# Which engine makes the first softmax-sum addition: a routed attention and mixture-of-experts kernel with one addition per group on GpSimd, an earlier transpose and one more drain

## The chip, the cores and the metric

One NeuronCore of a Trainium2 chip runs the whole kernel as one program. The metric is the device time of one execution in microseconds (us), taken as the median of several executions. The engines are TensorE (PE, with its weight loads as PEld), VectorE (DVE), ScalarE (ACT), GpSimd (POOL) and SyncE (SP, which here only issues DMAs). Each engine works through its own queue in order and waits on semaphores for the others.

## The reference

```python
# attention: 4 batches, 8 heads, 768 positions, head width 64, 16 clusters
q_assign = np.argmax(np.einsum('bhsd,hcd->bhsc', q_n, c_n), axis=-1)
k_assign = np.argmax(np.einsum('bhsd,hcd->bhsc', k_n, c_n), axis=-1)
mask = q_assign[:, :, :, None] == k_assign[:, :, None, :]
scores = np.where(mask, scale * np.matmul(q, k.transpose(0, 1, 3, 2)), -1e9)
attn = np.exp(scores - np.max(scores, axis=-1, keepdims=True))
attn = attn / (np.sum(attn, axis=-1, keepdims=True) + 1e-09)
x = heads_side_by_side(np.matmul(attn, v))                  # 3072 x 512

# router and experts: 8 experts, 512 -> 1024 -> 512
logits = xn @ en.T / tau
expert_idx = np.argmax(logits, axis=1)
gate_w = softmax(logits)[np.arange(N), expert_idx]
for e in range(E):
    mask = expert_idx == e
    h = np.maximum(x[mask] @ w1[e], 0.0)
    out[mask] = gate_w[mask, None] * (h @ w2[e])
```

A position attends only to the keys of its own cluster, and each of the 3072 rows goes through one expert.

## The kernel before

The order of instructions on all five engines is written out by hand: the program's order is the order of each queue.

**Attention** is done for 16 pairs of heads (4 batches, 4 pairs each, `n` from 0 to 15). A pair has two groups (the halves `hq` of its 768 queries) and a group has six units (`j`, 128 keys each). A unit's scores are computed by `scores` into a PSUM tile of two, `expo` exponentiates them on ACT into one of five `prob` buffers (128 x 768 values), and `attend` multiplies them with `v` into `o_ps`. The main loop takes two units at a time, so a pair has six iterations `it` (0 to 2 for the first group, 3 to 5 for the second). In each iteration the scores and exponentials of the next two units come before the attention products of the current two. An exponential therefore needs the buffer of the unit five places earlier, which both `attend`'s matmuls and its addition must have read.

The denominators are collected beside this. `attend` adds the `prob` tiles of a group up into `acc`: for `j == 1` one DVE instruction (L515) adds the first two and a small constant, and for each later unit another DVE instruction (L525) adds one more. When a group ends, ACT copies `o_ps` into `o_sb` (L530, one buffer), and `unite` adds its two halves into `o_sum` (L539) on POOL, in the last pair on DVE. This is done in iteration 2 for a pair's first group and in iteration 5 for its second. In iteration 0 of the next pair `total` (L553) sums `acc` over partitions on PE for both groups, and DVE and POOL turn and copy the reciprocals (L570, L571, L574). In iteration 2 `divide` transposes them (L585) and scales `o_sum` into `xT` (L589). `rows` (L606, L613) turns `xT` and writes it to memory in iteration 3.

Other work stands between these: the next pair's transposes of q and k (L386), its cluster choice (L405, L414 to L417, with ACT's L419 and L422), a batch's router products, logits and choice (L632, L644, `choose` from L680 on, with six small additions on POOL for running counts, L686), and, from batch 2 on, the placement of the rows of the first four expert blocks (`early`, for instance L864, L747, L931 and L934, and three gathers issued by POOL in iteration 3 of pair 14).

**Behind attention** the last batch's router runs between the first expert blocks. `products(0)` (L632, for the first half of the batch) is issued at the end of the loop, `products(1)` after the last group has been divided. Their results lie in PSUM tiles that `misc()` hands out in turn from two, and `logits` (L644) transposes each into `lt` on DVE. `total` of the last group takes the other tile between them. Then the experts follow: four early blocks, and 16 more items, `sized` ones (32-row pieces, gathered and scattered by POOL's indirect DMAs, L1041 and L1052) and blocks of 128 rows in turn. The last item is a block. Ahead of it `send` scatters the pieces of the sized item before it, and its own result is scattered last (L1288 on ACT, then L1052). At the end of the program every engine drains and meets the others.

Of the kernel before, what the change touches and what calls it, by code (L numbers as in the profile page):

```python
# [12 lines left out]
ALU = mybir.AluOpType  # L13
# [21 lines left out]
def bc(ap, shape, axis):  # L35
    return ap.unsqueeze(axis).to_broadcast(shape)
# [3 lines left out]
def kernel(  # L40
# [12 lines left out]
    nc = tc.nc  # L53
# [8 lines left out]
    HS = S // 2  # L62
# [118 lines left out]
    NP = len(pairs)  # L181
# [277 lines left out]
    un = [dict() for _ in units]  # L459
# [32 lines left out]
    def expo(i):  # L492
        d = un[i]
        d["prob"] = probs[i % len(probs)]
        nc.scalar.activation(d["prob"][:, :, 0:HS], d["s_ps"][:, :, 0:HS], ACTF.Exp, scale=scale)  # L495

    def attend(i):

        n, hq, j = units[i]
        d, g = un[i], gr[i // GU]  # L500
        if j == 0:
            g["o_ps"] = psO.tile([P, 2, 512], F32, tag="o_ps", name="o_ps")
        for h in range(2):
            for half in range(2):
                keys = slice(D * half, D * half + D)
                nc.tensor.matmul(  # L506
                    g["o_ps"][D * h : D * h + D, half, 0:HE],
                    lhsT=ld[n]["v"][keys, j, h],
                    rhs=d["prob"][keys, h, 0:HE],
                    start=(j == 0),  # L510
                    stop=(j == NJ - 1),
                )
        if j == 1:
            g["acc"] = xp.tile([P, 2, HS], F32, tag="acc", name="acc", bufs=3)
            nc.vector.scalar_tensor_tensor(  # L515
                out=g["acc"],
                in0=un[i - 1]["prob"][:, :, 0:HS],
                scalar=NJ * EPS,
                in1=d["prob"][:, :, 0:HS],
                op0=ALU.add,  # L520
                op1=ALU.add,
            )
            un[i - 1].clear()
        elif j > 1:
            nc.vector.tensor_tensor(g["acc"], g["acc"], d["prob"][:, :, 0:HS], ALU.add)  # L525
            d.clear()
        if j == NJ - 1:
            t = ld[n]
            t["o_sb"] = xp.tile([P, 2, HE], F32, tag="o_sb", name="o_sb", bufs=1)
            nc.scalar.copy(t["o_sb"], g["o_ps"][:, :, 0:HE])  # L530

    def unite(g):

        n, hq, _ = units[GU * g]
        t = ld[n]
        if hq == 0:
            t["o_sum"] = xp.tile([P, 2, HE], F32, tag="o_sum", name="o_sum", bufs=2)
        add = (nc.gpsimd if n + 1 < NP else nc.vector).tensor_tensor
        add(t["o_sum"][:, hq], t["o_sb"][:, 0], t["o_sb"][:, 1], ALU.add)  # L539
# [38 lines left out]
    def divide(*gs):  # L578
        n, hq, _ = units[GU * gs[0]]
        d = gr[gs[0]]  # L580
        G = len(gs)
        if hq == 0:
            xT[pairs[n]] = xp.tile([P, 2, HS], F32, tag="xT", name="xT", bufs=4)
        if G == 2:
            nc.vector.transpose(  # L585
                d["den"].rearrange("p k (u t) -> p (k u) t", t=SQ),
                bc(d["inv2"].rearrange("p k h u -> p (k h u)"), [P, G * HS // SQ, SQ], 2),
            )
        nc.vector.scalar_tensor_tensor(  # L589
            out=xT[pairs[n]][:, hq : hq + G],  # L590
            in0=ld[n]["o_sum"][:, hq : hq + G, 0:HS],
            scalar=ld[n]["o_sum"][:, hq, HS:HE],
            in1=d["den"],
            op0=ALU.add,
            op1=ALU.mult,
        )
        for g in gs:
            gr[g].clear()
# [486 lines left out]
    def weights2(it, parts=1):  # L1085
        for i in range(parts):
            load_part(w2s[it.slot], moe_w2, it.e, KF, i, parts)
# [152 lines left out]
    def send(it):  # L1240

        u0 = FIRST[it.j]
        for u in range(WIDE[it.j]):
            at = flat(spidx)[:, u0 + u : u0 + u + 1]
            scatter(out_pieces, at, mo[it]["ys"][:, u], NQ * N)
        del mo[it]

    def flat(t):
        return t.rearrange("p k w -> p (k w)")

    def hidden(it, halves=(0, 1)):

        d = mo[it]
        for half in halves:
            if half == 0:
                d["hT"] = mop.tile([P, F], F32, tag="hT", name="hT")
            f0 = 512 * half
            bk = psH.tile([P, 512], F32, tag="h_ps", name="h_ps")
            for m in range(0, 512, P):
                for c in range(KD):  # L1260
                    nc.tensor.matmul(  # L1261
                        bk[:, m : m + P],
                        lhsT=w1s[it.slot][:, c, f0 + m : f0 + m + P],
                        rhs=d["xT"][:, P * c : P * c + P],
                        start=(c == 0),
                        stop=(c == KD - 1),
                    )
            nc.scalar.activation(d["hT"][:, f0 : f0 + 512], bk, ACTF.Relu)  # L1268
# [133 lines left out]
    with tc.manual_schedule(engines=by_hand):  # L1402
        begin()
        for i in range(0, len(units), 2):
            n, it = divmod(i // 2, NJ)

            if n == it == 0:
                load(2, "qk")
            if it == 2 and n + 1 < NP:
                load(n + 1, "v")  # L1410
            if it >= 4 and n + 3 < NP:
                load(n + 3, "qk"[it - 4])
            for m in range(i + 2, min(i + 4, len(units))):
                scores(m)
                expo(m)
            between(n, it)
            if it == 4 and n == NP - 1:
                divide(2 * n)
            b, nb = divmod(n, NHP)
            if (b, nb, it) in early:  # L1420
                early[b, nb, it]()
            if i + 2 == len(units):
                ats.close()
                tile_waits = {"side": "right", "reuse_waits": "tile"}
                psX = ctx.enter_context(tc.tile_pool(name="psX", bufs=1, space=PSUM, **tile_waits))
                turn_x(E0[0], nc.scalar.copy, xp.tile([P, DM], F32, tag="acc", name="xTm", bufs=3))
            for m in range(i, i + 2):
                attend(m)
            if it == 2:
                if n > 0:  # L1430
                    divide(2 * n - 2, 2 * n - 1)
                unite(2 * n)
            elif it == 5:
                unite(2 * n + 1)
            if i + 2 == len(units):
                rows(ngroups - 2)
                route[b][0](0)
            if it == 0 and n > 0:
                total(2 * n - 2, 2 * n - 1)
            elif it == 3 and n == NP - 1:  # L1440
                total(2 * n)
# [10 lines left out]
        products, logits, read, norms, choose = route[B - 1]  # L1452
        pb = Places(1, rtb)
        gates = gate_pieces(0, B - 1)
        gates[0]()
        hidden(E0[0], (0,))
        order_x(E0[3])
        total(ngroups - 1)
# [7 lines left out]
        hidden(E0[0], (1,))  # L1466
        gates[3]()
        weights1(E0[2])
        logits(0)
        read(0, NJ, P - SQ, P)  # L1470
        products(1)
        hidden(E0[1], (0,))
# [82 lines left out]
        LAST = len(later) - 1  # L1555
        for i, it in enumerate(later):
            if i == LAST - 1:
                overflow()
                weights1(later[LAST])
                weights2(later[LAST])  # L1560
            if it.kind == "sized":
                order_w2(it)
            if i + 1 < len(later):
                turn_x(later[i + 1])
            if i > 0 and i + 2 < len(later) and later[i + 2].kind == "sized":
                fetch(later[i + 2])
            if i > 0 and later[i - 1].kind == "sized":
                send(later[i - 1])
            if it.kind == "sized":
                sized_hidden(it)  # L1570
            else:
                hidden(it)
            if i == 0:
                pb.gates(slot_gates)
            for j in range(i + 2, min(i + 4, len(later))):
                if later[j].kind == "block" and later[j] not in mo:
                    if it.kind == "sized":
                        nc.gpsimd.tensor_copy(pace, mo[it]["hT"][0:1, KF - 1, 0:1])
                        fetch(later[j])
            if i + 2 < LAST:  # L1580
                weights1(later[i + 2])
                if it.kind == "sized":
                    weights2(later[i + 2])
            if it.kind == "sized":
                sized_result(it)
            else:
                result(it)
            if i == 0:
                fetch(later[2])
                spread_gates()  # L1590
            if i + 2 < LAST and it.kind != "sized":
                weights2(later[i + 2])
# [45 lines left out]
```

## Time and profile before

| | us |
|---|---|
| median of 8 runs | 709.48 (709.26 to 710.89) |
| the profiled execution | 709.55 |
| its span, first to last instruction | 707.8 |
| PE busy in the span | 690.8 (98%) |
| DVE busy | 382.4 (54%) |
| ACT busy | 265.1 (37%) |
| POOL busy | 267.8 (38%) |
| granted TensorE clock, mean | 0.995 |

A row of a group names line, engine, operation, out<-in, partitions x elements and count, then busy time, mean ns of one, and the idle time of the engine before it with what ended it. A row of the timeline begins with the start and the duration in us; the brackets hold the idle time before it and its releaser. A table by stage gives, for each stretch, its length, the busy time of PE, PEld, DVE, ACT and POOL, the granted clock (1.00 is full), the share of the DMA engines and GB/s. An engine's name with a q is its sequencer, which waits, drains or issues. The mean shares hide the stages: attention runs to about 335 us, with DVE busy for 17 to 19 of every 20 us, and the experts from there to the end, with DVE mostly idle.

### The profile page before, as it was taken

To read this page: it belongs to the slowest core of one execution; us is meant where nothing else is said; L and a number is where in the kernel's file an instruction comes from. 1 tells how busy PE (TensorE), PEld (TensorE's weight loads), DVE (VectorE), ACT (ScalarE), POOL (GpSimd) and SP (SyncE) were. 2 spreads that over 40 slices of the span, in tenths; PEclk is the share of its full clock that TensorE was granted. 3 is DMA by queue.
4 is the path that set the end of the run, shared out by engine and by line. 5 is a ranking of instruction groups with operands and counts; after the bars stand their busy time and mean duration, and the time that the engine had idled before them with its cause. 6 is when DMAs were issued, how large, how long until landed. Compare 5 with 4: busy or idle time off the path is not lost.

```text
span 707.8 us, 16122 instructions
## 1 busy us (share of the span) xinstructions
PE 690.8 (98%) x6518; PEld 456.3 (64%) x6518; DVE 382.4 (54%) x665; ACT 265.1 (37%) x446; POOL 267.8 (38%) x402
## 2 busy tenths in 40 slices
PE   6999999999999999999899999999999999999995
PEld 3444444444444444455876668897979797979793
DVE  4788888989889999989484121340220303031210
ACT  4566655677566755576215110101011111111110
POOL 2122222322234222453213546736264554544412
PEclk9999999999999999999999999999999999999999
DMA  9536565786657688769788987268768686969450
GB/s 146 92 62 107 105 104 89 142 165 112 99 107 139 128 144 156 186 173 321 200 283 300 353 307 270 73 239 286 259 223 298 209 302 226 319 244 328 144 193 28
DMA packets 244124, 135.55 MB, mean 192 GB/s; under 512 B 207808, under 2 KB 207810, under 8 KB 244044
## 3 DMA queue, kind: packets, MB, share of 16 engines
q1 hardware_dynamic: 237852, 121.28, 64.0%
q0 software_dynamic: 6016, 13.12, 5.3%
q8 instruction: 54, 0.88, 0.6%
q14 instruction: 26, 0.21, 0.1%
q10 hardware_dynamic: 176, 0.05, 0.0%
HBM read 115.92 MB, written 13.12 MB: 182 GB/s over the span
## 4 chain that ended last, share of the span: by engine, by line
PE 80%; DVE 7%; DMA 5%; issue 4%; POOL 1%; SPq 1%; ACT 0%; POOLq 0%; DVEq 0%; ACTq 0%
PE s_ps L484 18%; PE o_ps L506 15%; PE h_ps L1261 10%; PE y_ps L1277 10%; PE h_ps L1176 9%; PE y_ps L1213 5%; PE misc L1213 5%; DMA out_dram<-ys,spidx 3%; PE x_ps L1176 3%; DVE acc L525 3%; PE misc L553 2%; PE misc L396 2%; DMA x_rows<-xb 1%; PE misc L632 1%; DMA k<-in_k_dram 1%
## 5 line engine op out<-in xcount | busy, mean ns | idle before, releaser
L495 ACT ACTIVATE prob<-s_ps 128x768 f32<-128x768 f32 x192 | 153.7, 812 | 95.0 <-PE s_ps L484 82.1
L484 PE MATMUL s_ps<-qT,kT 64*64 64x384 f32 x1536 | 156.0, 482 | 0.0
L506 PE MATMUL o_ps<-prob,v 64*64 64x385 f32 x1536 | 142.0, 486 | 0.0
L525 DVE TENSOR_TENSOR acc<-acc,prob 128x768 f32<-128x768 f32 x128 | 125.5, 981 | 8.8 <-ACT cd L422 0.5
L506 PEld LDWEIGHTS o_ps<-prob,v 64*64 64x64 f32 x1536 | 54.6, 133 | 70.3 <-issue 58.5
L1261 PE MATMUL h_ps<-xTm,w1s 128*128 128x128 f32 x768 | 90.0, 278 | 0.0
L1261 PEld LDWEIGHTS h_ps<-xTm,w1s 128*128 128x128 f32 x768 | 89.0, 195 | 1.4 <-issue 1.0
L1222 DVE STREAM_TRANSPOSE ys<-y_ps 128x256 f32<-128x256 f32 (+4 forms) x16 | 6.7, 417 | 153.4 <-PE y_ps L1213 153.4
L539 POOL TENSOR_TENSOR o_sum<-o_sb 128x385 f32<-128x385 f32 x30 | 32.0, 1068 | 144.1 <-ACT o_sb L530 144.1
L1052 POOL DMA_INDIRECT out_dram<-ys,spidx x56 | 56.9, 1017 | 74.7 <-DVE ys L1236 59.8
L1277 PE MATMUL y_ps<-w2s,hT 128*128 128x512 f32 x192 | 84.5, 593 | 0.0
L484 PEld LDWEIGHTS s_ps<-qT,kT 64*64 64x64 f32 x1536 | 56.0, 133 | 38.1 <-issue 34.9
L1176 PE MATMUL h_ps<-xTs,w1s 128*128 128x272 f32 (+7 forms) x384 | 72.9, 346 | 1.1 <-ACTq L1537 1.1
L1176 PEld LDWEIGHTS h_ps<-xTs,w1s 128*128 128x128 f32 x384 | 66.6, 190 | 8.0 <-issue 2.4
L1268 ACT ACTIVATE hT<-h_ps 128x512 f32<-128x512 f32 x24 | 14.3, 596 | 148.0 <-PE h_ps L1261 148.0
L484 PE MATMUL s_ps<-hot 64*64 64x384 bf16 x768 | 64.7, 325 | 2.2 <-ACT prob L495 1.1
L574 POOL COPY inv<-inv 32x12 f32<-32x12 f32 x120 | 45.5, 379 | 54.6 <-DVE inv L571 50.2
L1041 POOL DMA_INDIRECT xs<-x_rows,gpidx x56 | 57.4, 1026 | 17.1 <-issue 16.8
L1277 PEld LDWEIGHTS y_ps<-w2s,hT 128*128 128x128 f32 x192 | 35.6, 190 | 40.2 <-issue 40.2
L484 PEld LDWEIGHTS <-hot 64*64 64x64 bf16 x768 | 23.6, 106 | 39.4 <-issue 38.3
L1213 PE MATMUL y_ps<-hTs,w2o 128*128 128x272 f32 (+7 forms) x256 | 48.0, 346 | 0.0
L1213 PE MATMUL misc<-hTs,w2o 128*128 128x272 f32 (+7 forms) x256 | 48.0, 346 | 0.0
(264 smaller groups left out, 680.1 us busy)
## 6 DMA issues: line engine op xcount, KB each, us to landing
w1s<-in_moe_w_dram SPq DMA_DIRECT2D x18, 2048.0 KB, 11.1
w2s<-in_moe_w_dram SPq DMA_DIRECT2D x18, 2048.0 KB, 13.5
v<-in_v_dram SPq DMA_DIRECT2D x128, 48.0 KB, 2.3
q<-in_q_dram SPq DMA_DIRECT2D x60, 96.0 KB, 3.8
k<-in_k_dram SPq DMA_DIRECT2D x60, 96.0 KB, 3.7
x_rows<-xb SPq DMA_DIRECT2D x60, 96.0 KB, 2.7
xr<-x_rows SPq DMA_DIRECT2D x9, 512.0 KB, 3.9
w1s<-in_moe_w_dram SPq DMA_DIRECT2D x4, 1024.0 KB, 9.9
```

Source lines behind the costliest of these rows:

```text
L484: nc.tensor.matmul(s_ps[D * half : D * half + D, h, 0:HS], lhsT=l[rows, half], rhs=r[rows], start=part == (1 if len(parts) < 2 else 0), st ...
L495: nc.scalar.activation(d["prob"][:, :, 0:HS], d["s_ps"][:, :, 0:HS], ACTF.Exp, scale=scale)
L506: nc.tensor.matmul(g["o_ps"][D * h : D * h + D, half, 0:HE], lhsT=ld[n]["v"][keys, j, h], rhs=d["prob"][keys, h, 0:HE], start=(j == 0), st ...
L525: nc.vector.tensor_tensor(g["acc"], g["acc"], d["prob"][:, :, 0:HS], ALU.add)
L539: add(t["o_sum"][:, hq], t["o_sb"][:, 0], t["o_sb"][:, 1], ALU.add)
L574: nc.gpsimd.tensor_copy(inv2[M * to : M * to + M, :, i % 2], inv[M * i : M * i + M])
L1041: nc.gpsimd.indirect_dma_start(out=to, out_offset=None, in_=of, in_offset=bass.IndirectOffsetOnAxis(ap=at, axis=0), bounds_check=n - 1, oo ...
L1052: inst = nc.gpsimd.indirect_dma_start(out=to, out_offset=bass.IndirectOffsetOnAxis(ap=at, axis=0), in_=of, in_offset=None, bounds_check=n - 1,
L1176: nc.tensor.matmul(bk, lhsT=w1s[it.slot][:, c, P * f : P * f + P], rhs=d["xT"][:, c, 0:C], start=(c == 0), stop=(c == KD - 1),)
L1213: nc.tensor.matmul(bks[g][:, 0:C], lhsT=d["w2"][:, f, P * g : P * g + P], rhs=d["hT"][:, f, 0:C], start=(f == 0), stop=(f == KF - 1),)
L1261: nc.tensor.matmul(bk[:, m : m + P], lhsT=w1s[it.slot][:, c, f0 + m : f0 + m + P], rhs=d["xT"][:, P * c : P * c + P], start=(c == 0), stop ...
L1277: nc.tensor.matmul(bk, lhsT=d["hT"][:, P * c : P * c + P], rhs=w2s[it.slot][:, c], start=(c == 0), stop=(c == KF - 1),)
```

## The change

There are three independent parts.

1. The first addition of each group is done by POOL and without the constant; the second addition, on DVE, takes the constant over. `unite` of a group is issued later: for the first group of a pair in iteration 3 instead of 2, for the second in iteration 0 of the next pair instead of iteration 5, each time behind POOL's first addition of the following group. The last pair keeps its old places.
2. `logits(0)` of the last batch is issued right after the first gate piece behind the loop, before `total` and `divide` of the last group, where it used to stand behind them and the other gate pieces.
3. One drain of POOL is issued ahead of the last item, behind the scatters of the sized item before it.

```diff
         if j == 1:
             g["acc"] = xp.tile([P, 2, HS], F32, tag="acc", name="acc", bufs=3)
+            nc.gpsimd.tensor_tensor(
+                g["acc"], un[i - 1]["prob"][:, :, 0:HS], d["prob"][:, :, 0:HS], ALU.add
+            )
+            un[i - 1].clear()
+        elif j == 2:
             nc.vector.scalar_tensor_tensor(
                 out=g["acc"],
-                in0=un[i - 1]["prob"][:, :, 0:HS],
+                in0=g["acc"],
                 scalar=NJ * EPS,
                 in1=d["prob"][:, :, 0:HS],
                 op0=ALU.add,
                 op1=ALU.add,
             )
-            un[i - 1].clear()
+            d.clear()
         elif j > 1:
             nc.vector.tensor_tensor(g["acc"], g["acc"], d["prob"][:, :, 0:HS], ALU.add)
             d.clear()
...
-            if it == 2:
-                if n > 0:
-                    divide(2 * n - 2, 2 * n - 1)
+            if it == 0 and n > 0:
+                unite(2 * n - 1)
+            if it == 2 and n > 0:
+                divide(2 * n - 2, 2 * n - 1)
+            if it == (3 if n + 1 < NP else 2):
                 unite(2 * n)
-            elif it == 5:
+            elif it == 5 and n + 1 == NP:
                 unite(2 * n + 1)
...
         gates[0]()
+        logits(0)
         hidden(E0[0], (0,))
         order_x(E0[3])
         total(ngroups - 1)
...
         weights1(E0[2])
-        logits(0)
         read(0, NJ, P - SQ, P)
         products(1)
...
             if i > 0 and later[i - 1].kind == "sized":
                 send(later[i - 1])
+                if i == LAST:
+                    nc.gpsimd.drain()
```

## The prediction

> **What bounds the kernel now.** I read the page's chain of waits first. It runs through TensorE for 80% of the span, so what counts is where PE waits, not how busy an engine is.
>
> ```profile
> PE 80%; DVE 7%; DMA 5%; issue 4%; POOL 1%; SPq 1%; ACT 0%; POOLq 0%; DVEq 0%; ACTq 0%
> ...
> L525 DVE TENSOR_TENSOR acc<-acc,prob 128x768 f32<-128x768 f32 x128 | 125.5, 981 | 8.8 <-ACT cd L422 0.5
> ...
> L539 POOL TENSOR_TENSOR o_sum<-o_sb 128x385 f32<-128x385 f32 x30 | 32.0, 1068 | 144.1 <-ACT o_sb L530 144.1
> ```
>
> Next, the timeline of a typical pair of heads in attention. `total` (L553) starts at 79.07 and again at 98.40 us, so a pair takes 19.33 us, and PE runs without a gap in it; DVE is busy for 17 of 20 us there but late for nobody on PE.
>
> ```profile
> 82.80 4.17 DVE L525 TENSOR_TENSOR acc<-acc,prob 128x768 f32<-128x768 f32 x4
> 83.93 1.56 ACT L495 ACTIVATE prob<-s_ps 128x768 f32<-128x768 f32 x2 [0.17 <-PE s_ps L484]
> ...
> 92.65 1.56 ACT L495 ACTIVATE prob<-s_ps 128x768 f32<-128x768 f32 x2 [0.98 <-PE s_ps L484]
> 94.37 1.98 DVE L525 TENSOR_TENSOR acc<-acc,prob 128x768 f32<-128x768 f32 x2
> ...
> 98.40 0.88 PE L553 MATMUL misc<-acc,ones 128*32 128x192 f32 x16
> ```
>
> Only two pairs are stretched: the L553 starts at 237.14, 257.89 and 279.39 are 20.75 and 21.50 us apart. Less 19.33, and less the batch's router products in the second (some 1.6), 1.4 and 0.6 us remain. There PE waits for `acc` or for `prob` that DVE holds. So 2.0 us is all that a faster DVE can win.
>
> Third, behind attention, the only place where PE stands still for long:
>
> ```profile
> 339.03 3.74 PE L1261 MATMUL h_ps<-xTm,w1s 128*128 128x128 f32 x32
> 344.55 0.24 DVE L644 STREAM_TRANSPOSE lt<-misc 128x96 f32<-128x96 f32 x1
> 344.85 0.87 PE L632 MATMUL misc<-xT,embT 128*32 128x96 f32 x32 [2.08 <-DVE lt L644]
> 345.64 5.47 PE L1261 MATMUL h_ps<-xTm,w1s 128*128 128x128 f32 x32
> ...
> 346.00:348.00 2.00, 2.00 (x12) 2.00 (x11) 1.19 (x7) 0.00 (x0) 0.52 (x3) 0.50 0.02 2
> ```
>
> The last row is from the table by stage; its third number from the end is the granted clock, 0.50. The same 32 matmuls take 3.74 us before the gap of 2.08 and 5.47 behind it: the gap costs a second time.
>
> Last, the end of the program:
>
> ```profile
> L1633 POOLq DRAIN  x3: 40/113/6020, 700.9 to 707.5; - x3
> L1633 SPq DRAIN  x3: 7/7/13, 704.5 to 707.2; - x3
> 701.14 0.97 POOL L1052 DMA_INDIRECT out_dram<-y,sidx  x1 [7.40 <-ACT y L1288]
> ```
>
> GpSimd's closing drain takes 6.02 us, 700.9 to 706.9. SP, which waits for all DMAs, is through at 704.5. So the drain alone sets the last 2.4 us.
>
> **Logits turned sooner.** `products(1)` (L632) takes the PSUM bank that `logits(0)` (L644) reads, and L644 stands last of DVE's queue there. In the instruction listing of the changed kernel it stands before the reciprocal L562. Its input is ready at 334.05; DVE finishes `xb` at 336.66 and is idle until 338.65, so the 0.24 us costs nothing (without that idle time, 0.24). It issues no DMA and is moved past no other queue. PE then waits for `xT` alone, written at 341.87, before its matmuls end at 342.77: -2.08 us. The half clock goes with the gap: 5.47 - 3.74 = -1.73. The weights PE comes to sooner leave slack: issued at 347.12, moved by 355 (the GB/s by stage), needed at 362.2. Sum -3.8, certain to some 0.3 if the clock stays up.
> [...] This trace shows 0.50 behind a gap of 2.08, and the trace decides.
>
> **First addition on GpSimd.** 32 DVE instructions (L515, 0.94 us each in 30.1 us) go; the next addition takes over the constant; 32 additions of 128x768 come onto POOL. Their price is not in the trace. From L539 (0.86 us alone for 385 columns): in proportion 1.72, with the 0.19 of the smallest copies as a fixed part 1.53; L934's 528 bf16 columns in 1.59 give 2.3 in proportion. I take 1.65, nearest to L539; ends 1.5 and 2.3.
> [...]
>
> Dearer than its duration is whom it stops:
>
> ```profile
> 76.06 0.96 DVE L525 TENSOR_TENSOR acc<-acc,prob 128x768 f32<-128x768 f32 x1
> 76.30 1.44 POOL L539 TENSOR_TENSOR o_sum<-o_sb 128x385 f32<-128x385 f32 x1 [7.79 <-ACT o_sb L530]
> ...
> 86.97 0.86 POOL L539 TENSOR_TENSOR o_sum<-o_sb 128x385 f32<-128x385 f32 x1 [2.94 <-ACT o_sb L530]
> ...
> 135.79 2.62 DVE L525 TENSOR_TENSOR acc<-acc,prob 128x768 f32<-128x768 f32 x2
> 136.72 0.86 POOL L539 TENSOR_TENSOR o_sum<-o_sb 128x385 f32<-128x385 f32 x1
> ```
>
> Beside a DVE addition POOL ends 0.72 after DVE (77.74 against 77.02); where POOL was first, DVE's addition ends 0.83 after POOL (138.41 against 137.58). At 86.97 DVE ran a transpose and POOL was undisturbed. So additions of the two engines take turns, and each collision costs DVE POOL's whole time.
>
> Second group of a pair (iteration 3): its first two `prob` are there at 85.49, amid DVE's four additions, so DVE loses 1.65 - 0.13 = 1.5 and gains 0.94. First group: ready at 94.21, just before DVE's last two. In the worst order the chain is 1.65 (POOL) + 0.83 + 0.72 (`unite`, now behind it) + 0.83 = 4.03, so `acc` is done at 98.24; PE asks for it at 98.40. It fits by 0.16: ordinary pairs cost nothing, and if that cover goes, each tenth costs 15 pairs x 0.1 = 1.5 us. What `unite` feeds (L589 at 87.9) is behind the transpose L585 and not late. The gathers of pair 14, which stood behind `unite`, come ahead of both on POOL: 3 x 1.3 us from `gidx` at 305.65, done by 309.6, with the addition done at 311.2, as late as L515 is now (311.4).
>
> Where POOL or DVE is fuller it does not fit. Pairs 5, 9 and 13 put six `cumx` additions (3.76 us from 211.87) ahead of it on POOL: it starts at 215.63, DVE's last addition is held to 217.2 and ends at 218.0 where PE asks at 217.81: 0.2 x 3 = 0.6. At the end of pair 10 DVE comes 0.5 late (1.5 - 0.94), the addition starts at 234.0 and holds back L864, L747 and both last additions: 235.65 + 0.14 + 0.72 + 0.8 + 1.9 = 239.2 against 237.59 now, 1.6. Pair 11 has the same again with L934 ahead on POOL, but PE is then late as well, so its own stall of 1.4 is what DVE's lateness first fills: I take 1.4 for both. Sum +2.0. Ends: -2.0 (the stalls go, nothing collides on the path) and +9 (POOL at 2.3: 0.48 x 15 + 2.0).
>
> **One more drain.** It stands behind the five scatters of the last sized block, issued by 693.74; POOL idles to 701.14. At 6.02 or less it hides there, and holds up only the last scatter, which waits for ACT until 700.9. Rows: 0.04 to 0.19 us for the drains with no DMA before them, 6.02 for the one behind all. If the closing drain must clear what all earlier scatters left, it shrinks and SP's end at 704.5 sets the finish: -2.4. If the 4.8 us behind the last scatter belong to that one, 0. Neither row is nearer; I take -1.2.
>
> **Sum.** -3.8 + 2.0 - 1.2 = -3.0 us. The profiled execution took 709.55 (707.8 span and 1.75 around it): 706.55. The median shown is 0.07 below that execution: 706.5.
>
> **The rivals.** *DVE is really relieved*: collisions fall beside waits, the stalls of pairs 10 to 12 go, the drain gives all: -3.8 - 2.0 - 2.4 = -8.2, 701.3. For it: DVE waits for PE at 98 us with room to spare. Against: the two `prob` become ready just where DVE adds.
> *A wash*: the heavy pairs lose 3.6 and the drain gives nothing: 709.3. For it: pair 11's queue, with L934 ahead of the addition.
> *Slower, the shared turn becomes the bound*: in every pair the addition, `unite` and DVE's last two additions run in series behind the last exponential. At 2.3 us the chain is 4.68 against 4.19: 0.48 x 15 = 7.2, plus 2.0, less 3.8 = +5.4, 714.9. It decides from an addition of about 2.0 us, where attention loses more than 5.2. For it: L934's row. Against: L539's.
> *The drain does nothing, the rest as forecast*: 707.7, inside the forecast's own range.
>
> **How the numbers follow.** Forecast (own range 704.6 to 708.0) 0.52; DVE relieved 0.16; wash 0.15; slower 0.17. A measurement of this kernel tells about 0.2%, 1.4 us, from no change. Faster 0.68, same 0.15, slower 0.17. The range 702.8 to 710.8 leaves out part of the relieved case and most of the slow one, some 0.2.
>
> **What would show it.** Logits: L632 without a wait, the next 32 L1261 in 3.7 us, clock 1.0 at 346 to 348. Addition: POOL rows of 1.5 to 1.7 us alone, DVE additions of up to 2.4 us beside them, pairs at 19.33 us except 5, 9, 10, 11 and 13. Drain: the closing one ends with SP's. I am wrong if ordinary pairs stretch, if pairs 10 to 12 shorten, or if the half clock appears elsewhere.

## The result, and the profile after

The changed kernel takes 712.19 us (median; 710.81 to 714.05) where the kernel before takes 709.52 beside it: ratio 1.0036, 95% interval 1.0028 to 1.0045, so 2.0 to 3.2 us slower. The prediction was 706.5, with a range of 702.8 to 710.8: wrong in direction and outside the range. The profiled execution took 711.25 us, its span is 709.0 (before 709.55 and 707.8). Outside the span lie 2.2 us in this execution and 1.8 to 2.5 in the others of the changed kernel, against 1.7 to 1.9 before; no run shows why.

First the page of the changed kernel: the shares of the chain of waits, then groups of instructions (count | busy, mean ns of one | idle time of the engine before them).

```profile
PE 73%; DVE 12%; issue 6%; DMA 5%; POOL 2%; SPq 1%; ACT 1%; POOLq 0%; DVEq 0%; ACTq 0%
...
L530 DVE TENSOR_TENSOR acc<-acc,prob 128x768 f32<-128x768 f32 x96 | 131.8, 1373 | 8.7 <-DVE acc L530 0.5
L515 POOL TENSOR_TENSOR acc<-prob,prob 128x768 f32<-128x768 f32 x32 | 64.6, 2018 | 97.1 <-ACT prob L495 97.0
```

DVE made 32 additions fewer and was busy longer: 394.9 us against 382.4. The mean of its additions (L525 before, L530 now) went from 981 to 1373 ns, and its part of the chain from 7% to 12%. That is time in which DVE stands inside an instruction and waits for POOL: L530 takes 0.96 us (median) where no POOL instruction runs beside it, and up to 2.59 beside L515.

The next table takes four stretches of the trace. Attention runs from the first matmul into `o_ps` (L506) to the last; the next stretch ends where the second set of L1261 (now L1266) starts, behind the last batch's router products; then come the 32 matmuls of that set; the last one runs from the final scatter to the end.

| us | before | after | difference | predicted |
|---|---|---|---|---|
| attention | 313.69 | 321.44 | +7.75 | +2.0 |
| last `o_ps` matmul to second set of L1266 | 12.88 | 10.73 | -2.15 | -2.08 |
| the 32 L1266 behind it (half clock) | 5.47 | 3.84 | -1.63 | -1.73 |
| start of the last scatter to the end | 6.63 | 4.22 | -2.41 | -1.2 |

Together +1.6; attention began 0.3 us earlier in this execution, and the span grew by 1.3. The medians lie 2.7 us apart, these two executions only 1.7: the half clock of the third row, which the profiled execution before had, is in only some executions of that kernel (last section).

The logits did what was said. The timeline of the changed kernel (start and duration in us, engine, line, operation), and below it its table by stage (the granted clock is the third number from the end):

```profile
344.86 0.24 DVE L649 STREAM_TRANSPOSE lt<-misc 128x96 f32<-128x96 f32 x1
...
350.16 0.87 PE L637 MATMUL misc<-xT,embT 128*32 128x96 f32 x32
```
```profile
348.00:350.00 2.00, 2.00 (x20) 2.00 (x19) 1.93 (x4) 0.58 (x1) 0.00 (x0) 1.00 1.12 169
350.00:352.00 2.00, 2.00 (x44) 1.73 (x43) 1.44 (x6) 0.81 (x2) 0.00 (x0) 1.00 0.39 59
```

The PSUM tile is read out into `lt` by 345.10, 5.1 us before L637 (L632 before) starts, which has no wait any more, and PE is busy without a gap at full clock.

The drains of the changed kernel, from the listing by line (shortest/median/longest in ns, first and last start), the closing one and the added one:

```profile
L1642 POOLq DRAIN  x3: 46/113/2943, 704.6 to 708.8; - x3
L1642 SPq DRAIN  x3: 7/13/25, 708.1 to 708.7; - x3
```
```profile
L1577 POOLq DRAIN  x1: 8892/8892/8892, 693.3 to 693.3; - x1
```

The closing drain fell from 6.02 to 2.94 us and is through at 707.5; SP's at 708.1 now sets the end. The added one lasts 8.9 us, to 702.2, beside PE's last block. A part of each is waiting for scatters: the last one ahead of the added drain ends at 697.42, so 4.7 us of that drain follow it, as 4.8 us followed the last scatter in the kernel before; behind the last scatter only 1.7 us of the closing drain now remain.

The loss is all in attention. An ordinary pair, and the end of pair 9 with the start of pair 10, both from the timeline of the changed kernel:

```profile
94.23 1.83 POOL L515 TENSOR_TENSOR acc<-prob,prob 128x768 f32<-128x768 f32 x1 [5.17 <-ACT prob L495]
94.86 3.54 DVE L530 TENSOR_TENSOR acc<-acc,prob 128x768 f32<-128x768 f32 x2
96.01 1.58 POOL L544 TENSOR_TENSOR o_sum<-o_sb 128x385 f32<-128x385 f32 x1
98.34 1.00 PE L558 MATMUL misc<-acc,ones 128*32 128x192 f32 x16
...
216.80 3.57 DVE L530 TENSOR_TENSOR acc<-acc,prob 128x768 f32<-128x768 f32 x2
217.74 1.81 POOL L515 TENSOR_TENSOR acc<-prob,prob 128x768 f32<-128x768 f32 x1
218.00 1.78 PE L506 MATMUL o_ps<-prob,v 64*64 64x385 f32 x16
220.29 0.57 DVE L405 STREAM_TRANSPOSE asn<-misc 128x384 f32<-128x384 f32 x1
220.91 0.88 PE L558 MATMUL misc<-acc,ones 128*32 128x192 f32 x16 [1.13 <-DVE asn L405]
```

At 94 us the four additions go POOL, DVE, POOL, DVE in turn, end at 98.40, and PE's sum over partitions (L558) starts at 98.34 and is stretched from 0.88 to 1.00: a loss of 0.12. At 217 us POOL has had the six `cumx` additions to make first. L515 starts at 217.74, DVE's last addition is held until 219.55 and ends at 220.37, the transpose L405 stands behind it, and PE waits.

The step from the first to the second iteration of a pair (between the first L506 matmuls) shows it; an undisturbed pair takes 3.90 us (the last one 3.85), and pairs that are not listed did not change there.

| pair | 2, 3, 4, 7 | 6 | 10 | 11 | 12 | 13 | 14 | 15 |
|---|---|---|---|---|---|---|---|---|
| first step before | 3.90 | 3.90 | 3.97 | 4.41 | 4.49 | 3.90 | 3.90 | 3.85 |
| first step after | 4.02 | 5.18 | 5.36 | 5.73 | 5.21 | 4.21 | 5.17 | 4.58 |
| whole pair, longer by | 0.12 each | 1.29 | 1.55 | 0.41 | 0.72 | 0.36 | 1.96 | 0.74 |

With 0.07 in pair 5 and 0.18 in pair 9 these are the 7.75 us.

### The profile page after: what moved, and what is told of

Its sections match the earlier page's. It is cut to its first block, busy times and chain, and to the rows that moved or that the text cites. A ratio compares the mean times of both kernels' runs of the same rounds, so it can differ in the third digit from the quotient of the medians.

```text
span 709.0 us, 16144 instructions
## 1 busy us (share of the span) xinstructions
PE 692.0 (98%) x6518; PEld 455.8 (64%) x6518; DVE 394.9 (56%) x633; ACT 264.9 (37%) x446; POOL 342.2 (48%) x434
## 4 chain that ended last, share of the span: by engine, by line
PE 73%; DVE 12%; issue 6%; DMA 5%; POOL 2%; SPq 1%; ACT 1%; POOLq 0%; DVEq 0%; ACTq 0%
PE s_ps L484 14%; PE o_ps L506 11%; PE h_ps L1266 10%; PE y_ps L1282 10%; PE h_ps L1181 9%; DVE acc L530 5%; PE misc L1218 5%; PE y_ps L1218 5%; DMA out_dram<-ys,spidx 3%; PE x_ps L1181 3%; PE misc L558 2%; PE misc L396 1%; DVE acc L520 1%; DMA x_rows<-xb 1%; PE misc L637 1%
## 5 line engine op out<-in xcount | busy, mean ns | idle before, releaser
L506 PE MATMUL o_ps<-prob,v 64*64 64x385 f32 x1536 | 142.2, 486 | 0.0
L530 DVE TENSOR_TENSOR acc<-acc,prob 128x768 f32<-128x768 f32 x96 | 131.8, 1373 | 8.7 <-DVE acc L530 0.5
L515 POOL TENSOR_TENSOR acc<-prob,prob 128x768 f32<-128x768 f32 x32 | 64.6, 2018 | 97.1 <-ACT prob L495 97.0
L506 PEld LDWEIGHTS o_ps<-prob,v 64*64 64x64 f32 x1536 | 55.0, 133 | 70.1 <-issue 58.7
L1266 PE MATMUL h_ps<-xTm,w1s 128*128 128x128 f32 x768 | 88.3, 275 | 0.0
L1266 PEld LDWEIGHTS h_ps<-xTm,w1s 128*128 128x128 f32 x768 | 87.4, 192 | 1.4 <-issue 1.0
L579 POOL COPY inv<-inv 32x12 f32<-32x12 f32 x120 | 43.0, 359 | 37.9 <-DVE inv L576 33.5
```

Source lines behind the costliest of these rows:

```text
L506: nc.tensor.matmul(g["o_ps"][D * h : D * h + D, half, 0:HE], lhsT=ld[n]["v"][keys, j, h], rhs=d["prob"][keys, h, 0:HE], start=(j == 0), st ...
L515: nc.gpsimd.tensor_tensor(g["acc"], un[i - 1]["prob"][:, :, 0:HS], d["prob"][:, :, 0:HS], ALU.add)
L579: nc.gpsimd.tensor_copy(inv2[M * to : M * to + M, :, i % 2], inv[M * i : M * i + M])
L1266: nc.tensor.matmul(bk[:, m : m + P], lhsT=w1s[it.slot][:, c, f0 + m : f0 + m + P], rhs=d["xT"][:, P * c : P * c + P], start=(c == 0), stop ...
```

## The experiments

The first four ran on a chip on which the kernel before took 712.31 us, the others on two with 709.5; each ratio is to the kernel before on its own chip. "Attention" is the stretch of the table above: 313.7 us before, and 314.2 in executions whose first pair took 0.5 longer.

### Each part alone

`e1_logits` is the kernel before with the earlier `logits(0)` only, `e2_drain` with the drain only, `e3_attention` with the POOL additions and the later `unite` only, `e4_logits_drain` has the first two. Their diffs are the parts of the change itself.

> Only the earlier logits(0). If the half clock belongs to PE's gap of 2.08 us, both go: -2.1 - 1.7 = -3.8 us against the kernel before, and the 32 L1261 behind the gap take about 3.75 us. Rival: the half clock comes from something else at that place (the weights arriving, the change of stage) and only the gap goes: -2.1 us, with a stretch at clock 0.5 still in the expert blocks.

Ratio 0.9957 (0.9942 to 0.9973), -3.1 us (-4.1 to -1.9). The stretch to the second set of L1261 is 10.73 us, and the clock stays at 1.00 behind it. Both halves of the expectation hold in the profile; the time comes out smaller, though its interval still holds -3.8. The likely reason is in the last section.

> Only the additional drain. If the closing drain pays for the scatters of the whole program, it falls from 6.0 to about 2.9 us and the end comes 2.4 us sooner. Rival: it pays for the last scatter alone, stays near 6 us, and the time does not move (0 +- 0.5 us).

Ratio 0.9969 (0.9955 to 0.9982), -2.2 us. The closing drain takes 2.95 us, last scatter to end 4.23. These are the numbers of the first theory; whether it is scatters that are paid for is taken up below.

> Only the first additions on POOL with the later unite. Theory (additions of the two engines take turns, and 1.83 us on POOL are lost to DVE where it is already full): attention ends 7 to 8 us later, time +7.5 us against the kernel before. Rival (as predicted, with the rest of the loss in a disturbance between the three parts): +2 us.

Ratio 1.0116 (1.0096 to 1.0135), +8.3 us; attention 321.46, step for step that of the changed kernel. The loss belongs to this part alone; the two others do not disturb it.

> Earlier logits and the drain, first additions left on DVE. If the parts are independent, -3.8 - 2.4 = -6.2 us against the kernel before, about 703.3 us. Rival: the parts get in each other's way (the drain was hidden by the later end of the expert blocks), and less than 4.5 us come.

Ratio 0.9928 (0.9916 to 0.9941), -5.1 us (-6.0 to -4.2). Attention is as before (314.1), both gains are there. The parts add up: -3.1 - 2.2 + 8.3 = +3.0, and the whole change has +2.6. This version beats both kernels.

### Which part of the attention change costs

`e5_unite_only` leaves all additions on DVE and takes only the later `unite`. `e6_add_old_unite` has the additions on POOL and `unite` in its old places. `e7_second_groups` and `e8_first_groups` give POOL the first addition in one group of each pair only; the diff is that of `e7_second_groups` against the changed attention:

```diff
-        if j == 1:
+        if j == 1 and hq == 1:
...
-        elif j == 2:
+        elif j == 2 and hq == 1:
...
+        elif j == 1:
+            g["acc"] = xp.tile([P, 2, HS], F32, tag="acc", name="acc", bufs=3)
+            nc.vector.scalar_tensor_tensor(
+                out=g["acc"],
+                in0=un[i - 1]["prob"][:, :, 0:HS],
+                scalar=NJ * EPS,
...
```

In the other groups DVE makes the addition as in the kernel before; in `e8_first_groups` the condition is `hq == 0`.

> All additions stay on DVE, only unite is issued at its later places; logits and drain as before. Theory (the POOL addition between two DVE additions is what costs): attention, from the first o_ps matmul to the last, as before, 313.9 +- 0.5 us, time within 0.2% of the kernel before. Rival (the later unite holds DVE's last addition or delays what reads o_sum): attention 1 to 3 us longer.

Ratio 1.0004 (0.9992 to 1.0017), attention 314.25 with the longer first pair, every other step within 0.06 us of before. Moving `unite` costs nothing.

> First addition on POOL only in the second group of each pair, later unite for all. Theory: nothing in the middle of a pair has an end that PE asks for, so +0 to +1.5 us, and that in pairs 10 to 14 alone. Rival (DVE's load as a whole): half of the loss, +3 to +4.

Ratio 1.0022 (1.0010 to 1.0034); the time, +1.6 us (0.7 to 2.4), is near the theory's; attention is 316.1, +2.4 us, outside both expectations. It lies in pairs 6 (0.31), 10 (0.59), 14 (1.00, of it 0.69 in its fifth step) and a few tenths elsewhere.

> First addition on POOL only in the first group of each pair, later unite for all. Theory: nearly the whole loss, +5.5 to +7.5 us, with the first step of pairs 6, 10 and 14 at about 5.2 instead of 3.9 us. Rival: half of it, +3 to +4.

Ratio 1.0090 (1.0073 to 1.0107); the time, +6.4 us, is the theory's, but 1.3 us of the profiled execution come from a later start of attention (last section). Attention itself is 318.4, +4.7, again between the two. Pair 6 takes 4.68 in its first step, pair 10 4.97, pair 14 4.67. So the first groups cost two thirds and the second groups one third, and the two nearly add up in the same places (7.15 of 7.75 us). Here is pair 6 in `e5_unite_only` and then in `e8_first_groups` (timeline):

```profile
137.32 2.62 DVE L525 TENSOR_TENSOR acc<-acc,prob 128x768 f32<-128x768 f32 x2
138.26 0.86 POOL L539 TENSOR_TENSOR o_sum<-o_sb 128x385 f32<-128x385 f32 x1
138.72 1.52 PE L506 MATMUL o_ps<-prob,v 64*64 64x385 f32 x16
140.17 0.88 PE L553 MATMUL misc<-acc,ones 128*32 128x192 f32 x16
```
```profile
137.63 3.58 DVE L541 TENSOR_TENSOR acc<-acc,prob 128x768 f32<-128x768 f32 x2
138.57 1.83 POOL L515 TENSOR_TENSOR acc<-prob,prob 128x768 f32<-128x768 f32 x1
139.03 1.52 PE L506 MATMUL o_ps<-prob,v 64*64 64x385 f32 x16
141.27 0.88 PE L569 MATMUL misc<-acc,ones 128*32 128x192 f32 x14 [0.27 <-DVE acc L541]
```

In the first, DVE's last addition of the group was already held by `unite` (0.86 us) and ended at 139.94, 1.22 us after L506 began. In the second it is held by L515 (1.83) and ends at 141.21, 2.18 after it: 0.96 later, the difference of the two POOL instructions. PE begins its sum 1.45 us after L506. One rule gives all four kernels: the first step is 3.90 us plus whatever the addition ends later than 1.40 us after L506's start (the 1.40 is fitted to these rows).

| | first addition on POOL in | addition ends after L506 | rule | measured |
|---|---|---|---|---|
| `e5_unite_only` | no group | 1.22 | 3.90 | 3.90 |
| `e7_second_groups` | second | 1.72 | 4.22 | 4.21 |
| `e8_first_groups` | first | 2.18 | 4.68 | 4.68 |
| `e3_attention` | both | 2.68 | 5.18 | 5.18 |

The 0.50 of the second group is DVE's lateness, carried on through a queue with hardly any idle time: from the fourth iteration of pair 5 to its end DVE idles for 0.3 us in `e7_second_groups`, nowhere more than 0.11 at a time.

> First additions on POOL, unite at its old places, so that POOL's queue has unite (which waits for o_sb) ahead of the addition of a pair's first group. Theory (it costs because the addition starts before DVE's last two additions of the old group and holds them): the addition now starts behind unite, DVE's last two are through, and the loss falls from 7.5 to at most 3 us. Rival (POOL's 1.83 us are lost to DVE wherever they fall, because DVE is full in attention): the loss stays at 6 to 8 us.

Ratio 1.0152 (1.0128 to 1.0176), attention 321.9, +8.2: the number is the rival's, the places are the theory's. Pairs 1 to 4, 7 and 8 are at 3.90 and 19.33 (20.92) us; pairs 6 and 10 take 4.22 and 4.40 in their first steps, as with second groups alone, so the first groups there cost nothing once the addition stands behind `unite`. The loss has moved: 1.6 us in pair 11 and 4.6 in pair 14. The timeline of pair 14, and below it two windows of the table by stage:

```profile
312.15 1.26 POOL L544 TENSOR_TENSOR o_sum<-o_sb 128x385 f32<-128x385 f32 x1 [3.42 <-ACT o_sb L535]
313.58 1.25 POOL L1046 DMA_INDIRECT xin<-x_rows,gidx  x1 [0.17 <-DVE den L590]
...
317.45 1.82 POOL L515 TENSOR_TENSOR acc<-prob,prob 128x768 f32<-128x768 f32 x1
319.30 0.81 ACT L495 ACTIVATE prob<-s_ps 128x768 f32<-128x768 f32 x1 [3.58 <-POOL acc L515]
```
```profile
316.70:320.12 3.42, 1.05 (x16) 0.41 (x9) 0.82 (x1) 0.82 (x2) 3.10 (x3) 1.00 1.03 288
320.12:323.53 3.41, 3.37 (x24) 1.66 (x27) 3.10 (x4) 2.11 (x4) 0.00 (x0) 0.50 0.90 200
```

`unite` holds POOL's queue until `o_sb` is there, the three gathers come behind it, then L515, and ACT waits 3.58 us for the `prob` buffer that L515 reads. PE, starved by it, is busy for 1.05 us of a window of 3.42, and the next 3.41 us run at half clock: up to 1.7 of the 4.6 us are this, and not the queue itself. The changed kernel has the same queue without `unite` in front, and loses 0.69 there.

### Size and order of the addition

`e9_half` gives POOL only the columns of the first head:

```diff
-            nc.gpsimd.tensor_tensor(
-                g["acc"], un[i - 1]["prob"][:, :, 0:HS], d["prob"][:, :, 0:HS], ALU.add
-            )
+            for h, eng in enumerate((nc.gpsimd, nc.vector)):
+                eng.tensor_tensor(
+                    g["acc"][:, h], un[i - 1]["prob"][:, h, 0:HS], d["prob"][:, h, 0:HS], ALU.add
+                )
```

> As e3 (later unite, logits and drain as before), but POOL makes only the half of the first addition that belongs to the first head (128x384), DVE the other. Theory (DVE's addition is held for as long as POOL's lasts): POOL's half takes about 0.9 us, the chain at the end of an ordinary pair is 3.3 instead of 4.2 us, ordinary pairs are back at 3.90 for the first step, and attention loses 1.5 to 3.5 us instead of 7.5. Rival (each hand-over between the engines has its price, whatever the size): 6 us or more stay.

Ratio 1.0031 (1.0015 to 1.0048); attention 315.18, +1.5. All ordinary pairs are back at 3.90 us, pair 6 takes 4.17, pair 10 4.37. The loss goes with the addition's length (1.24 us on the mean here, 2.02 in the changed kernel), and faster than in proportion, since the slack swallows the rest. DVE makes 32 half additions more here (574 ns each), so its load is not what costs.

`e11_held` keeps the full additions and the later `unite` and changes only when they can start; `e12_held_all` is the changed kernel with the same lines.

```diff
             g["acc"] = xp.tile([P, 2, HS], F32, tag="acc", name="acc", bufs=3)
+            if i > GU:
+                seen = smp.tile([1, 1], F32, tag="seen", name="seen", bufs=1)
+                nc.gpsimd.tensor_copy(seen, gr[i // GU - 1]["acc"][0:1, 1, HS - 1 : HS])
             nc.gpsimd.tensor_tensor(
```

> As e3, with one copy of a single element on POOL ahead of each first addition that reads the last value of the previous group's acc: the addition can start only when DVE has made its last addition of the group before. Same additions, same places of unite. Theory (the loss is the order: the addition gets ahead of DVE's last two): the first steps of pairs 2 to 10 are back at 3.90 to 4.1 us and attention loses less than 2.5 us; DVE's additions of that stage take about 0.95 us again. Rival (POOL's time is lost to DVE wherever it falls, or the additions now come too late for the prob buffers): 5 us or more stay.

Ratio 1.0033 (1.0019 to 1.0047), +2.3 us; attention 315.19, +1.5 in place of +7.75. Between span and time lie 2.0 to 2.6 us here (1.7 to 1.9 before), so 0.2 to 0.8 of the 2.3 lie outside the span. Pairs 1 to 10 are at 3.90 us without exception. The groups of this kernel:

```profile
L533 DVE TENSOR_TENSOR acc<-acc,prob 128x768 f32<-128x768 f32 x96 | 92.1, 960 | 8.7 <-DVE acc L533 0.5
L518 POOL TENSOR_TENSOR acc<-prob,prob 128x768 f32<-128x768 f32 x32 | 58.0, 1812 | 12.8 <-ACT prob L495 12.8
```

The same 32 additions lie on POOL, and 31 of them have a copy ahead. But DVE's additions take 960 ns instead of 1373, and POOL's 1812 instead of 2018. So it is the order that costs, not the work. What is left lies in pair 11 (one step of 4.61 us for 3.40, where ACT waits 2.46 us for DVE's L417, 1.30 before), pair 14 (0.82: ACT waits 1.81 us for the addition behind the gathers) and pair 15 (0.14); pairs 10 and 12 are 0.08 and 0.15 shorter than before.

> The changed kernel with that copy ahead of each first addition. Theory: -3.8 - 2.4 from the logits and the drain and 0 to +2 from attention, 703.5 to 705.5 us where the kernel before has 709.5, and at best level with the version without any POOL addition. Rival (as for the held additions alone): 709 to 712.

706.83 us, ratio 0.9965 (0.9954 to 0.9976): 2.5 us faster than the kernel before and above what was expected; the ratios of `e1_logits`, `e2_drain` and `e11_held` give -3.1 - 2.2 + 2.3 = -3.0. It stays behind the version without any POOL addition (0.9928, on another chip; 0.9949 for `e10_drain_earlier` below, on this one): attention takes 315.2 us here and 313.7 there, so freeing DVE of 30 us brought attention nothing.

### What the closing drain waits for

`e10_drain_earlier` is `e4_logits_drain` with the drain two items earlier (`LAST - 2`).

> Earlier logits and the drain, first additions on DVE, the drain two items earlier (behind the scatters of the sized item before the last one), so that five more scatters and the last block's predecessor lie between it and the end. If the closing drain's length goes with the scatters since the last drain, it is between 2.9 and 6.0 us, and part of the 2.4 us is lost; if any drain anywhere behind the gathers will do, it stays at 2.9.

```profile
L1570 POOLq DRAIN  x1: 9912/9912/9912, 653.5 to 653.5; - x1
L1635 POOLq DRAIN  x3: 46/113/3196, 696.9 to 701.1; - x3
```

Behind the added drain lie 7 of the 68 scatters and no gather (1 in `e4_logits_drain`), and the closing drain takes 3.20 us; last scatter to end is 4.23 as in `e4_logits_drain`, because SP's drain sets the end. Ratio 0.9949 (0.9930 to 0.9967), not told apart from 0.9928. Behind the last scatter 2.0 us of the closing drain remain (1.7 with the later drain, 4.8 without one). So it pays mainly for what lies far back, and the place of the added one matters little. What it clears the trace does not say: all gathers and most scatters lie ahead of both added drains, and nothing tells them apart from a price of the first such drain.

## Why the prediction was wrong

**What bounds the kernel: right as far as the runs go.** "2.0 us is all that a faster DVE can win" was not exceeded: in `e11_held`, with 32 additions off DVE and no collision, the first steps of pairs 10 to 12 fall to 3.90, 3.90 and 4.01 us, 1.1 us in all, but the third steps of pairs 11 and 12 take 1.5 back.

**Logits: right in place and mechanism, not in certainty.** The gap went (-2.15 measured, -2.08 predicted) and with it the half clock. But the 1.73 us of half clock were counted as sure ("certain to some 0.3 if the clock stays up"). They are there in some executions only (last section). `e1_logits` has -3.1, with an interval that does not exclude -3.8; what decides here is the profiles of the last section.

**Drain: between my two readings I took the middle, -1.2; the full 2.4 came** (`e2_drain` -2.2). Of the two mechanisms, `e2_drain` and `e10_drain_earlier` rule out that the last scatter alone costs it. That it is earlier scatters that the closing drain clears, they allow but do not show.

**First addition on GpSimd: this term failed, +2.0 against +7.75.** The collision was right: the two engines' additions take turns, and DVE's is held for POOL's whole time (L530 took 2.55 us at the end of pair 9, L525 there 1.59), and the 0.5 us of lateness from the second group was measured as 0.50. What the collisions cost PE was not:

- Ordinary pairs: said "nothing", measured 0.12 in four of them, 0.5 in all. The chain took 4.17 us instead of 4.03, because the addition takes 1.83 alone instead of 1.65. From its start (94.23) to PE's sum (98.34) there were 4.11 in this execution, not 4.19, and PE's second matmul there started 0.06 us after DVE's end, a hand-over that the chain left out. So the slack of 0.16 was gone.
- **The step that broke it: "held to 217.2 and ends at 218.0 where PE asks at 217.81: 0.2 x 3 = 0.6"** for the pairs with `cumx` in front. Measured 1.28, 1.39 and 1.27, together 3.9. By its own figures it should have read 215.63 + 1.65 + 0.83 = 218.11, or 0.3 a pair, but two larger things were wrong in it. First, 217.81 is not when PE asks; its weight load was already waiting there, for L405, which stands behind that addition on DVE and frees the PSUM tile. The row of the kernel before says so:

```profile
217.81 0.51 PEld L553 LDWEIGHTS misc<-acc,ones 128*32 128x32 f32 x16 [0.67 <-DVE asn L405]
```

  In the kernel before that addition ended at 217.26; L405 and the hand-over to PE fill the 0.55 us to 217.81. There was no slack in pair 10 and 0.18 us in pairs 6 and 14 (by the rule above), so the difference between the old holder (`unite`, 0.86) and the new one (1.83), 0.96, went onto PE almost whole: `e8_first_groups` has 0.94 in pair 10 and 0.78 and 0.77 in pairs 6 and 14, against `e5_unite_only`. Second, the 0.5 us by which the second group's addition makes DVE late was worked out, and then counted for pairs 10 and 11 only. DVE has hardly any idle time in which to lose it, so it arrives in these pairs too (`e7_second_groups`, against `e5_unite_only`: 0.31 to 0.37); even the `cumx` additions start later by it, since they wait for DVE's `eq`.
- Ends of pairs 10 and 11: said 1.4, measured 1.1 (pairs 11 and 12). Right: their first steps lost 2.0 us together, and 0.9 us of pair 11's own stall, in its later steps, went in return, as was foreseen.
- Not foreseen: 2.2 us. Pair 14's gathers ahead of L515 were costed as "as late as L515 is now"; `gidx` was ready at 311.7, the gathers started at 312.56 and not at once, the addition ended at 318.36, 6.7 us behind `gidx` and not the 5.55 counted on, and ACT, which needs the buffer that it reads, came late (0.69). Pairs 13 and 15 (1.1) and small parts of pairs 5, 9 and 10 make the rest; no run tells their causes apart, but in `e11_held` only 0.15 us of the 1.1 is left.

**The rival on the slow side had the mechanism and not the place.** It let every pair stretch from an addition of 2.0 us on. The addition is shorter than that, ordinary pairs hardly stretch, and attention still loses 7.75, in the pairs where POOL or DVE has more to do. Its 714.9 was nearer than the forecast.

## What to carry to other kernels

Before work is moved to an engine whose instructions take turns with the old one's (here L515 on POOL with 1.83 us alone and L530 on DVE with 0.96), look at what order the two queues will interleave in where a deadline ends: an instruction that becomes ready early gets ahead of the old engine's last ones and holds them for its full length (2.55 us for L530 at the end of pair 9), while the same instruction, made to wait for them by a copy of one element, cost 1.5 us in place of 7.75. Slack is to be read per pair and from what the waiting engine's row names as its releaser; a start time that is itself the end of a wait, as 217.81 in pair 10, has no slack. A lateness on an engine with hardly any idle time (DVE idles for 0.3 us in the second half of pair 5) is paid at the next deadline, wherever that lies, and not only where it arose: of the 0.50 us from the second groups, 0.31 to 0.37 came up in pairs 6, 10 and 14.

## What the runs showed of the hardware

**In these runs the half clock depends on where the gap falls in a fixed grid of 3.41 us.** The same gap of 2.08 us in front of L632 is in nine of the profiles; five have a half-clock stretch behind it (the kernel before, `e3_attention`, `e6_add_old_unite`, `e8_first_groups`, `e11_held`), four have none (`e2_drain`, `e5_unite_only`, `e7_second_groups`, `e9_half`). Where an execution has several half-clock stretches of this kind, they begin at distances of whole multiples of 3.413 us: in the kernel before the one behind the gap runs from 345.94 to 349.36 us, and the next begins at 704.34, 105.0 such lengths after it; in `e8_first_groups` three begin, by its table by stage, at 16.80, 351.32 and 709.72, 98.0 and 105.0 lengths apart. Laid out from them, the windows of the kernel before and then of `e9_half` read as follows (PE's busy time is the second number, the granted clock the third from the end):

```profile
342.53:345.94 3.41, 1.33 (x37) 1.00 (x36) 1.86 (x9) 0.81 (x2) 0.00 (x0) 1.00 0.44 65
345.94:349.36 3.42, 3.42 (x18) 3.42 (x17) 1.25 (x7) 0.00 (x0) 1.20 (x6) 0.50 0.28 50
```
```profile
341.96:345.37 3.41, 1.95 (x18) 1.76 (x16) 2.81 (x9) 1.11 (x3) 0.00 (x0) 1.00 0.66 97
345.37:348.79 3.42, 2.80 (x50) 2.66 (x51) 1.94 (x10) 0.00 (x0) 0.24 (x2) 1.00 0.25 38
```

In all five with the half clock the gap lies whole in one window, PE is busy for 1.33 of 3.41 us there, and the next window has clock 0.50. In all four without it a boundary cuts the gap, no window has more than 1.47 us idle, and the clock stays at 1.00. A sixth case is pair 14 of `e6_add_old_unite` above, with 1.05 us busy. So the part worth 1.73 us is drawn by lot in each execution, and removing the gap removes the lot. In one window of 3.41 us, 2.08 us of idle time were enough for the half clock; 1.47 at this place, and 1.75 in the kernel before at 14.85 to 18.26 us, were not.

The same lot is drawn at the start: eight of the fourteen profiles have a half-clock stretch at 16 to 21 us, and in those the first `o_ps` matmul starts at 20.0 to 20.4 us, in the others at 18.7 to 19.1. This alone moves an execution by some 1.3 us. Two such lots fit the spread of the kernel before: of its 25 executions beside `e9_half` to `e12_held_all`, four took 707.6 to 708.0 us at a mean clock of 0.997, fourteen 708.7 to 709.7 at 0.994 or 0.995, and seven 710.4 to 710.8 at 0.993.

**A tiny instruction was held as long as a large one.** In `e6_add_old_unite` L752, an instruction on 1x32 values, starts just behind POOL's L515 at the end of pair 10, takes 1.76 us and ends 0.05 after it; the instructions behind it, with 1x4 results, take 0.16 to 0.17:

```profile
237.91 1.83 POOL L515 TENSOR_TENSOR acc<-prob,prob 128x768 f32<-128x768 f32 x1
238.03 1.76 DVE L752 TENSOR_TENSOR picka<-whicha,io_f 1x32 f32<-1x32 f32 x1
239.82 0.17 DVE L753 TENSOR_REDUCE numa<-picka 1x4 f32<-1x32 f32 x1
```

So L752 was held for some 1.6 us, as L530 was in the changed kernel (up to 2.59 us, 0.96 without POOL beside it). What it is in the two instructions that makes the engines take turns, no run shows.
